# Pool fills an unread tile behind each indirect transfer while the chunks run; the scratch for dynamic transfers is halved

## The chip, the cores and the metric

The kernel runs on one core of one Trainium2 chip. The metric is the device time of the whole program in microseconds (us). PE is the matrix engine (TensorE), DVE the vector engine, ACT the scalar engine, POOL the GpSimd engine; SP issues most of the plain DMA transfers, and POOL issues the indirect ones, whose rows are picked by indices that lie in SBUF.

## What is computed

A long convolution by FFT, gated by x, and then a routed expert layer over the resulting 45824 tokens of width 128 (four sequences of 11456):

```python
def _attn_ref(x, v, pos_emb, w1, w2):
    h_filt = (np.maximum(pos_emb @ w1, 0.0) @ w2) * window        # filter of length S
    u = x * v
    y = irfft(rfft(u, 2 * S) * rfft(h_filt, 2 * S))[:, :S]        # along the sequence
    return x * y

def _moe_ref(x, w_skip, w_gate, w1, w2):
    out = x.copy()
    do_compute = x @ w_skip > 0
    xc = x[do_compute]
    logits = xc @ w_gate                                          # 8 experts
    e_idx = np.argmax(logits, axis=1)
    gate_w = softmax(logits)[e_idx]
    for e in range(E):
        h = np.maximum(xc[mask_e] @ w1[e], 0.0)                   # 128 -> 1024
        y[mask_e] = gate_w[mask_e, None] * (h @ w2[e])            # 1024 -> 128
    out[do_compute] = xc + y
```

Everything is float32.

## The kernel before

The program has four stretches. `first_phase` multiplies x by v, makes the filter and does the first step of the forward transforms. `freq_phase` does the second step, the product in the frequency domain and the first step of the inverse. `out_phase` does the last inverse step in 32 **chunks** of three blocks each, gates the result, stores it to `out` in HBM, scores every token and works out its place in a list of its expert. `late_slots` runs the experts.

A **slot** is 256 tokens of one expert, in two halves of 128. A slot needs three kinds of indirect transfers, and POOL issues all of them:

- `name` (L652): its 256 row numbers are fetched from `lists` into `ids`. One transfer.
- `gather` (L686): its rows of `out` are fetched into a buffer `xt`, 129 numbers a row. Two transfers, one for each half.
- `store` (L757): its results in a buffer `o` are written back to the rows of `out`. Two transfers.

The 29 **early slots** (`early_slots`) run inside `out_phase`, beside the chunks: a generator yields after each piece of work, and the loop over chunk steps resumes it once or more in a step. `late_slots` runs the rest after the chunks, partly two slots at a time. The order on each engine is written out by this code (the schedule is manual), so every engine works through a fixed list. For an early slot that is: turn the gathered rows (`turn_high`, PE transposes at L740 into a PSUM tile `mh`), multiply by the expert's first weights (`up`, L751 to L753), ReLU on ACT (L774), multiply by the second weights (L823), gate (`gated`, DVE at L763), two stores on POOL, then the `name` and `gather` transfers of later slots. Between them stand the chunk's own instructions: the inverse step (L1066) and its gating (`xm`, DVE at L1067), PE transposes (L1079, L1093), scores (L1087, copied out by ACT at L1089), and the routing (L1132 to L1194).

```python
for n in range(s, min(s + GATHERS, XT - 1 + s)):    # how far gathers run ahead
    if n not in got and n in self.names:
        got[n] = self.gather(n, self.ids[:, n], pool, self.names[n])
```

A gather is so issued as soon as its slot is named and lies within 12 slots ahead. POOL has no other work than indirect transfers from the start of the chunks on.

The scratch for dynamic transfers is a part of SBUF that the program sets aside at the start of each partition; unless it is said otherwise it is 16384 bytes. The kernel's tiles lie behind it.

The functions that the change touches, and what calls them:

Of the kernel before, what the change touches and what calls it, by code (L numbers as in the profile page):

```python
# [12 lines left out]
F16 = mybir.dt.float16  # L13
# [45 lines left out]
NLATE = 64  # L59
NLAST = NEARLY + NLATE - NKNOWN  # L60
NTAB = 188


def units():
# [11 lines left out]
def tables():  # L76
# [70 lines left out]
        "cols": (col[:, None] < col[None, :]).astype(np.float16), "odd": odd.astype(np.float16),  # L147
        "iota": np.tile(np.arange(NTAB, dtype=f), (X.stop, 1)),
        "shift": at64(shift).astype(np.float16), "bump": at64(bump.reshape(E, 1)).astype(f),
# [3 lines left out]
class First:  # L153
# [42 lines left out]
    def store(self):  # L196

        for dst, xs in self.late:
            self.nc.sync.dma_start(dst, xs)
        self.late = []  # L200
# [115 lines left out]
def freq_phase(tc, nc, i, fi, zd, c3, spare, loads):  # L316
# [9 lines left out]
    with (  # L326
# [116 lines left out]
        for n in range(ALL + LAG):  # L443
# [18 lines left out]
            begin(n + 1, 0)  # L462
            step()
            store()
            if n < ALL:
                half(1)
# [5 lines left out]
            if n < ALL:  # L472
                nc.gpsimd.tensor_tensor(y[:, 1:], y[:, 1:], p1, ALU.add)  # L473
                nc.gpsimd.tensor_tensor(y[:, 2:], y[:, 2:], p2, ALU.add)  # L474
            back(2)
        store(nc.scalar)


class Experts:
# [7 lines left out]
    def __init__(self, tc, i, out, lists, mc, wf):  # L487
# [10 lines left out]
        nc.vector.memset(self.ones, 1.0)  # L498
        self.iota = mc.tile([nx, NTAB], F32, name="iota")
        nc.sync.dma_start(self.iota, i["iota"])  # L500
        self.first = mc.tile([nx, NTAB], F16, name="first")
        nc.vector.memset(self.first, 0.0)
# [15 lines left out]
        nc.sync.dma_start(self.parts, i["parts"].rearrange("p (a b) -> p a b", a=2))  # L518
        self.past = mc.tile([nx, NTAB], F32, name="past")
        nc.vector.memset(self.past, 0.0)  # L520
# [4 lines left out]
        nc.vector.memset(self.counts, 0.0)  # L525
        self.tab = mc.tile([1, NKNOWN + NTAB], I32, name="tab")
        self.total = mc.tile([1, 1], I32, name="total")
# [12 lines left out]
    def table(self, counts, last, base, limit, unit, pool, keep, ps):  # L540
# [3 lines left out]
        nc = self.nc  # L544
        mm = nc.tensor.matmul
        col = lambda name, dt=F32: pool.tile([X.stop, 1], dt, name=name)[X]
        NC1 = 2 * E + 1
        shift, incl = self.shift[X, 0], self.shift[X, 1]
# [3 lines left out]
        mm(ps[X, C:C + 1], shift, done, start=True, stop=True)  # L552
        mm(ps[0:C, NTAB:NTAB + NC1], counts, self.sums[:, 0:NC1], start=True, stop=True)
        yield
# [89 lines left out]
    def sum(self, ps, pool, name="at"):  # L644
        at = pool.tile([128, 1], I32, name=name)
        with self.nc.allow_low_precision(reason="whole numbers that float32 holds"):
            self.nc.vector.tensor_reduce(at, ps, axis=AX.X, op=ALU.add)  # L647
        return at

    def name(self, at, ids, have=H2):  # L650

        self.nc.gpsimd.indirect_dma_start(  # L652
            out=ids, out_offset=None, in_=self.lists[0:have * PP],
            in_offset=bass.IndirectOffsetOnAxis(ap=at, axis=0), bounds_check=have * PP - 1, oob_is_err=False)

    def issue(self, one):
        s, at, ch = one
        self.name(at, self.ids[:, s], ch + 1)
        self.names[s] = ch

    def group(self, ins, name, *others):

        for g in others:
            self.tc.declare_no_dep(ins.ins, group=g, reason="they have rows of their own")
        self.tc.add_to_no_dep_group(name, ins.ins)
# [12 lines left out]
    def gather(self, s, ids, pool, since=None):  # L678

        nc = self.nc  # L680
        tb = self.entry(s, pool)
        self.held = (self.held + 1) % len(self.xts)
        xt = self.xts[self.held]
        have = 128 * NS * (H2 if since is None else since + 1)
        for j in range(2):
            ins = nc.gpsimd.indirect_dma_start(  # L686
                out=xt[:, j], out_offset=None, in_=self.rows[0:have],
                in_offset=bass.IndirectOffsetOnAxis(ap=ids[:, j:j + 1], axis=0),
                bounds_check=have - 1, oob_is_err=False)
            self.group(ins, "gathers", "outs", *(f"rows{c}" for c in self.stored if since is not None and c > since))  # L690
        return tb, xt, ids, since

    def space(self, pool):


        nc = self.nc
        self.xts, self.held = [pool.tile([128, 2, W], F32, name=f"xt{k}", bufs=1) for k in range(XT)], 0
        self.o, self.at = [pool.tile([128, 2, W], F32, name=f"o{k}", bufs=1) for k in range(4)], 0
        for t in self.xts + self.o:
            nc.vector.memset(t, 0.0)  # L700
        self.reaches, self.turns = [pool.tile([LP + 1, T2], F16, name=f"reach{k}", bufs=1) for k in range(4)], 0
        for t in self.reaches:
            nc.vector.memset(t, 0.0)
            nc.vector.tensor_copy(t[LP:], self.slotpos[LP:])
# [50 lines left out]
    def store(self, o, ids, j, since=None):  # L755
        nc = self.nc
        ins = nc.gpsimd.indirect_dma_start(  # L757
            out=self.rows, out_offset=bass.IndirectOffsetOnAxis(ap=ids[:, j:j + 1], axis=0),
            in_=o, in_offset=None, bounds_check=H2 * 128 * NS - 1, oob_is_err=False)
        self.group(ins, "outs", "outs", "gathers", *(f"rows{c}" for c in self.stored if since is not None and c > since))  # L760

    def gated(self, o, y, xt, j):
        self.nc.vector.scalar_tensor_tensor(o, y, xt[:, j, D:D + 1], xt[:, j, 0:D], ALU.mult, ALU.add)  # L763

    def early_slots(self, pool, work, psum, bank):
# [25 lines left out]
        def prepare(s):  # L791

            while not all(n in self.names for n in unit(s)):
                yield
            gather(s)
            if s not in hl:
                for _ in range(4):
                    yield
                    gather(s)
                w[s] = self.split(got[s][0], pool, 0, nc.vector)  # L800
                hl[s] = self.turn([got[n] for n in unit(s)], pool, bank512())
                yield
                yield
# [31 lines left out]
    def late_slots(self, pool, queue):  # L835
# [3 lines left out]
        nc, tc = self.nc, self.tc  # L839
        with (  # L840
# [40 lines left out]
            def leave(sts, yt):  # L881
# [4 lines left out]
                for n, (tb, xt, ids, since) in enumerate(sts):  # L886
                    o = self.row()
                    for j in range(2):
                        self.gated(o[:, j, 0:D], tp[:, n * T + j * 128:n * T + (j + 1) * 128], xt, j)
                        self.store(o[:, j], ids, j)  # L890

            st, w, h = self.ahead
            w1, hl = {0: w.pop(NEARLY)}, {0: h.pop(NEARLY)}
            count = len(UNITS)
# [100 lines left out]
def out_phase(tc, i, out, zd, ex, consts):  # L995
# [6 lines left out]
    with (  # L1002
# [3 lines left out]
      with (  # L1006
# [267 lines left out]
        for ch in range(NCH):  # L1274
            for blk in range(NB):
                for lag, rank, f in ((0, 0, produced), (1, 4, turn), (2, 4.9, score), (3, 2, score2), (STORE, 9, store)):
                    steps.setdefault(first(ch) + blk + lag, []).append((rank, f, (ch, blk)))
            for lag, order, f in (
                    (6, 3, choose), (7, 1, exp), (7, 4.5, count), (7, 6, counted), (7, 6, gate), (8, 4.4, total),
                    (9, -2.5, even), (9, 0.5, spreadcounts), (9, 4.5, ranks),  # L1280
                    (10, -2, routed), (11, 3, spread), (12, 4.5, collect), (13, -3, write)):
                steps.setdefault(first(ch) + lag, []).append((order, f, (ch,)))
# [103 lines left out]

# [9 lines left out]
```

## Time and profile before

| | |
|---|---|
| three runs | 1799.66, 1805.27, 1805.89 us; median 1805.27 us |
| the profiled execution | 1805.72 us, of which the span of its instructions is 1803.8 us |
| busy share of the span | PE 88%, DVE 66%, POOL 56%, ACT 46% |
| indirect transfers | 186 gathers, 186 stores, 93 names |
| of these from 815 to 1340 us | 82 gathers, 58 stores, 60 names |

In the profile, a group's row gives line, engine, operation, out<-in, the count, then busy time and mean duration in ns, and behind the second bar the engine's idle time just before it with what ended it. In a row of the timeline stand the start, the duration, and in brackets the idle time before it and what ended it; "remote" stands there where the profile finds no recorded instruction that ended shortly before the release. A row of stretches gives for each engine the busy time and the number of instructions, then the granted clock of PE (1.00 is full speed), the busy share of the DMA engines and GB/s.

### The profile page before, as it was taken

The page shows a single profiled execution, that of the slowest core. Times are in us where ns is not written, and L with a number is a line of the kernel's source. Part 1 is how long each engine was busy: PE and PEld are TensorE (multiplying, and loading weights), DVE is VectorE, ACT ScalarE, POOL GpSimd, SP SyncE. Part 2 cuts the span into 40 slices and gives each one's busy share as a digit, 9 for nine tenths or more (in the row PEclk, how much of TensorE's full clock was granted, in tenths as well). Part 3 has the DMA queues.
Part 4 walks back from the last instruction along what each step waited for, and adds up shares of the span by engine and source line. Part 5 has one row for each costly group of instructions (what it writes and reads, how often), then busy time and mean ns, then how long its engine had stood idle before and what let it go on. Part 6 is the DMA issues. An engine that isn't in the chain of part 4 may idle for free. (4 is left out here: it accounts for less than half of the span.)

```text
span 1803.8 us, 26628 instructions
## 1 busy us (share of the span) xinstructions
PE 1589.3 (88%) x8528; PEld 1009.3 (56%) x8528; DVE 1198.3 (66%) x2524; ACT 822.6 (46%) x1740; POOL 1012.6 (56%) x664
## 2 busy tenths in 40 slices
PE   6987999999999999687789778979768898899897
PEld 2543444444444444234566556756656776787896
DVE  1326778887887999477566545756656665577685
ACT  3553545455454444233344334535424554455664
POOL 1005888888887888203453432234565676677563
PEclk9987999999999999899899889989889998999899
DMA  7999999999997898798566645755211111111110
GB/s 257 321 347 337 375 381 363 347 321 331 346 323 256 227 340 222 213 334 249 162 214 183 211 141 188 229 172 179 72 22 26 34 40 36 34 40 36 28 35 19
DMA packets 188665, 360.34 MB, mean 200 GB/s; under 512 B 54794, under 2 KB 128988, under 8 KB 188516
## 3 DMA queue, kind: packets, MB, share of 16 engines
q1 hardware_dynamic: 169484, 318.63, 52.6%
q0 software_dynamic: 18144, 38.67, 7.5%
q10 hardware_dynamic: 896, 1.32, 0.3%
q8 instruction: 69, 1.13, 0.3%
q14 instruction: 72, 0.59, 0.1%
HBM read 215.50 MB, written 144.11 MB: 199 GB/s over the span
## 5 line engine op out<-in xcount | busy, mean ns | idle before, releaser
L757 POOL DMA_INDIRECT out<-o,ids x186 | 210.8, 1133 | 352.7 <-DVE o L763 292.6
L413 PE MATMUL ps<-y,c 128*128 128x512 f32 x720 | 331.7, 597 | 2.1 <-POOL y L473 1.4
L473 POOL TENSOR_TENSOR y<-y,p 128x2048 f32<-128x2048 f32 x60 | 272.2, 4537 | 70.8 <-DVE p L402 70.8
L686 POOL DMA_INDIRECT xt<-out,ids x186 | 191.8, 1031 | 77.3 <-issue 50.9
L861 DVE SCALAR_TENSOR_TENSOR hh<-hp,hh 128x1024 fp32r<-128x1024 f32 x128 | 155.9, 1218 | 116.8 <-ACT hh L860 94.9
L413 PEld LDWEIGHTS ps<-y,c 128*128 128x128 f32 x720 | 133.3, 190 | 175.3 <-issue 155.0
L402 DVE TENSOR_TENSOR p<-xp,g 128x1024 f32<-128x1024 f32 x240 | 217.4, 947 | 0.0
L402 DVE TENSOR_TENSOR y<-xp,g 128x1536 f32<-128x1536 f32 x120 | 210.7, 1756 | 4.1
L860 ACT ACTIVATE hh<-hp 128x1024 fp32r<-128x1024 f32 x128 | 131.9, 1031 | 135.9 <-PE hp L753 51.2
L414 ACT COPY z<-ps 128x512 f32<-128x512 f32 x180 | 105.5, 586 | 178.7 <-PE ps L413 167.4
L652 POOL DMA_INDIRECT ids<-lists,at x93 | 101.0, 1086 | 125.1 <-DVE at L647 97.7
L751 PE MATMUL hp<-hl,ws 128*128 128x512 f32 (+1 forms) x336 | 126.4, 376 | 28.3 <-DVE hh L861 13.3
L728 DVE TENSOR_TENSOR ws<-wf,ws 128x1024 fp32r<-128x1024 f32 x113 | 137.5, 1217 | 12.7 <-ACT ws L723 7.1
L474 POOL TENSOR_TENSOR y<-y,p 128x1024 f32<-128x1024 f32 x60 | 141.4, 2357 | 4.7
L823 PEld LDWEIGHTS bank<-wd,h 128*128 128x128 f32 x928 | 122.0, 212 | 36.5 <-issue 36.5
L823 PE MATMUL bank<-wd,h 128*128 128x128 f32 x928 | 133.3, 302 | 1.1 <-issue 1.1
L1066 PE MATMUL y<-zt,c 128*64 128x512 f32 x384 | 115.4, 665 | 15.7 <-issue 9.5
L1067 DVE TENSOR_TENSOR xm<-y,ox 128x512 f32<-128x512 f32 x96 | 66.5, 692 | 93.6 <-PE y L1066 47.5
L211 PE MATMUL ps<-wf,c 60*120 60x384 f32 x512 | 112.4, 534 | 11.6 <-DVE wf L194 11.2
L382 PE MATMUL xp<-x,wf 128*128 128x480 f32 x256 | 115.7, 576 | 7.1 <-issue 3.8
L723 ACT CAST ws<-wf 128x1024 fp32r x113 | 118.0, 1044 | 7.3 <-issue 1.8
L752 PE MATMUL hp<-hl,ws 128*128 128x512 f32 (+1 forms) x336 | 118.1, 351 | 1.0 <-issue 1.0
(188 smaller groups left out, 3102.9 us busy)
## 6 DMA issues: line engine op xcount, KB each, us to landing
wf<-xv SPq DMA_DIRECT2D x64, 768.0 KB
zt<-zd SPq DMA_DIRECT2D x64, 768.0 KB
x1d<-wf SPq DMA_DIRECT2D x64, 720.0 KB
x<-x1d SPq DMA_DIRECT2D x60, 768.0 KB
zd<-z SPq DMA_DIRECT2D x118, 384.0 KB
out<-xm SPq DMA_DIRECT2D x96, 258.0 KB
ox<-xo SPq DMA_DIRECT2D x96, 256.0 KB
x1f<-fx POOLq DMA_DIRECT2D x16, 720.0 KB
```

The costliest lines, as they stand in the source:

```text
L402: nc.vector.tensor_tensor(o[:, :, :, j * KH:(j + 1) * KH].rearrange("p s a k b d -> p (s a) k b d"), x[:, None].broadcast_to([128, m, KH, ...
L413: nc.tensor.matmul(zps, c3[:, a, :], y[:, blk, a], start=(a == 0), stop=(a == 1))
L473: nc.gpsimd.tensor_tensor(y[:, 1:], y[:, 1:], p1, ALU.add)
L474: nc.gpsimd.tensor_tensor(y[:, 2:], y[:, 2:], p2, ALU.add)
L686: ins = nc.gpsimd.indirect_dma_start(out=xt[:, j], out_offset=None, in_=self.rows[0:have], in_offset=bass.IndirectOffsetOnAxis(ap=ids[:, j ...
L728: eng.tensor_tensor(w[:, 1], src[:, ds(self.where(eng, tb), F)], w[:, 0].bitcast(F32), ALU.subtract)
L751: nc.tensor.matmul(hp, w[:, 0, c], hl[:, 0], start=True, stop=False)
L752: nc.tensor.matmul(hp, w[:, 0, c], hl[:, 1], start=False, stop=False)
L757: ins = nc.gpsimd.indirect_dma_start(out=self.rows, out_offset=bass.IndirectOffsetOnAxis(ap=ids[:, j:j + 1], axis=0), in_=o, in_offset=Non ...
L823: nc.tensor.matmul(bank[:, j * D:(j + 1) * D], h[f // 2][:, f % 2, j * 128:(j + 1) * 128], wd[s][:, f * D:(f + 1) * D], start=(f == 0), st ...
L860: nc.scalar.activation(h[:, 0], hp, AF.Relu)
L861: nc.vector.scalar_tensor_tensor(h[:, 1], hp, 0.0, h[:, 0].bitcast(F32), ALU.max, ALU.subtract)
```

## The change

A method `pause` has POOL fill a tile `idle` of 128 partitions x 512 half-precision numbers with zeros. Nothing reads that tile. `pause` is called behind every `name`, `gather` and `store` transfer, as long as the flag `apart` is set: it is set at the start of `out_phase` and cleared near the start of `late_slots`, ahead of the first late fetch. The scratch for dynamic transfers is set to 8192 bytes, half of what it was.

```diff
+IDLE = 512
 ...
         self.nc.gpsimd.indirect_dma_start(
             out=ids, out_offset=None, in_=self.lists[0:have * PP], ...)
+        self.pause()
+
+    def pause(self):
+
+        if self.apart:
+            self.nc.gpsimd.memset(self.idle, 0.0)
 ...
             self.group(ins, "gathers", "outs", ...)
+            self.pause()
         return tb, xt, ids, since
 ...
+        self.idle, self.apart = pool.tile([128, IDLE], F16, name="idle", bufs=1), True
         self.reaches, self.turns = [pool.tile(...) for k in range(4)], 0
 ...
         self.group(ins, "outs", "outs", "gathers", ...)
+        self.pause()
 ...
+            self.apart = False
             st, w, h = self.ahead
 ...
-    nc = bacc.Bacc("TRN2", target_bir_lowering=False, num_devices=1)
+    nc = bacc.Bacc("TRN2", target_bir_lowering=False, num_devices=1, dynamic_dma_scratch_size=8192)
```

The order of instructions on PE, DVE, ACT and SP stays as it was, and so do their waits but for a few on ACT. On POOL 207 fills are added, 67 behind names, 82 behind gathers and 58 behind stores. The first fill waits for PE once (its memory was used before); every other one waits for the fill before it.

POOL in the middle of the chunks, before: the stores of an early slot, a name, the gathers of three slots ahead, two names, and the next slot's stores. `o`, `xt` and `at` are the buffers of results, gathered rows and list positions; L757 is a store, L686 a gather, L652 a name.

```order
L757 DMA out<-o_4457,ids 49152x129 x2
L652 DMA ids<-lists,at_8131 128x2
L686 DMA xt_4446<-out,ids 128x129 x2
L686 DMA xt_4447<-out,ids 128x129 x2
L686 DMA xt_4448<-out,ids 128x129 x2
L652 DMA ids<-lists,at_8209 128x2
L652 DMA ids<-lists,at_8211 128x2
L757 DMA out<-o_4458,ids 49152x129 x2
```

The same place after, as far as the second gathered slot. The lines of the code have moved: L766 is a store, L693 a gather, L653 a name, L661 the fill.

```order
L766 DMA out<-o_4457,ids 49152x129
L661 MEMSET idle 128x512
L766 DMA out<-o_4457,ids 49152x129
L661 MEMSET idle 128x512
L653 DMA ids<-lists,at_8204 128x2
L661 MEMSET idle 128x512
L693 DMA xt_4446<-out,ids 128x129
L661 MEMSET idle 128x512
L693 DMA xt_4446<-out,ids 128x129
L661 MEMSET idle 128x512
L693 DMA xt_4447<-out,ids 128x129
L661 MEMSET idle 128x512
```

Nothing changes places; a fill stands behind each transfer.

POOL where the late slots begin, before: two names, then the first late fetches and stores.

```order
L652 DMA ids<-lists,at_12690 128x2
L652 DMA ids<-lists,at_12692 128x2
L686 DMA xt_4442<-out,ids 128x129 x2
L757 DMA out<-o_4457,ids 49152x129 x2
L757 DMA out<-o_4458,ids 49152x129 x2
```

The same place after:

```order
L661 MEMSET idle 128x512
L653 DMA ids<-lists,at_12876 128x2
L661 MEMSET idle 128x512
L653 DMA ids<-lists,at_12878 128x2
L661 MEMSET idle 128x512
L693 DMA xt_4442<-out,ids 128x129 x2
L766 DMA out<-o_4457,ids 49152x129 x2
L766 DMA out<-o_4458,ids 49152x129 x2
```

The last fill stands behind the last name that `out_phase` issues; from there on POOL's list is as before.

## The prediction

> **What bounds the kernel now.** I read the page's busy times first, then the rows of stretches for the stretch that the change touches, then the same rows cut at the early slots, and last the timeline of the worst of them.
>
> ```profile
> PE 1589.3 (88%) x8528; PEld 1009.3 (56%) x8528; DVE 1198.3 (66%) x2524; ACT 822.6 (46%) x1740; POOL 1012.6 (56%) x664
> 815.00:1340.00 525.00, 427.28 (x3622) 318.41 (x3622) 320.97 (x1239) 218.81 (x519) 211.99 (x200) 0.91 0.55 172
> 1340.00:1803.00 463.00, 410.57 (x2276) 351.32 (x2275) 305.87 (x456) 239.59 (x293) 291.64 (x266) 0.95 0.13 32
> ```
>
> In a row of a stretch the length comes first, then busy time of PE, PEld, DVE, ACT and POOL, PE's granted clock, the DMA share and GB/s. PE is the bound: 88% of the span. The chunks with the early slots run from about 815 to 1340 us, where PE is idle 525 − 427.3 = 97.7 us and its clock is granted at 0.91. POOL is busy 212 us there, all of it with indirect transfers, and idle 313.
>
> Where PE's time goes is seen when the stretch is cut at the first transposes of successive early slots (L740). The first three rows below are slots whose seven or eight transfers stand apart; the next is the same work with two transfers; the last seven are the slots with bursts.
>
> ```profile
> 1222.28:1238.61 16.33, 14.65 (x132) 10.74 (x132) 10.74 (x44) 7.91 (x19) 7.30 (x8) 1.00 0.60 180
> 1238.61:1254.01 15.40, 14.28 (x132) 10.58 (x131) 10.64 (x43) 7.71 (x19) 7.60 (x7) 1.00 0.66 219
> 1254.01:1269.61 15.60, 13.80 (x132) 10.54 (x131) 10.46 (x41) 8.07 (x20) 7.64 (x8) 1.00 0.22 69
> 1154.58:1169.28 14.70, 14.70 (x138) 10.78 (x139) 12.78 (x50) 7.49 (x19) 2.55 (x2) 1.00 0.72 236
> 860.42:883.88 23.46, 16.93 (x135) 12.41 (x135) 12.34 (x48) 8.11 (x19) 12.41 (x12) 0.93 0.60 190
> 883.88:903.87 19.99, 18.08 (x133) 12.95 (x134) 10.66 (x43) 7.91 (x19) 4.01 (x4) 0.74 0.41 118
> 937.02:959.54 22.52, 17.67 (x126) 12.60 (x126) 10.06 (x34) 7.94 (x19) 11.91 (x12) 0.84 0.57 180
> 1004.75:1029.07 24.32, 14.13 (x131) 10.52 (x131) 12.48 (x49) 7.64 (x19) 15.63 (x15) 0.89 0.67 198
> 1029.07:1053.55 24.48, 16.31 (x128) 12.40 (x128) 10.36 (x35) 8.06 (x20) 9.05 (x9) 0.78 0.50 140
> 1053.55:1074.08 20.53, 15.33 (x121) 11.82 (x121) 7.85 (x28) 7.75 (x20) 7.12 (x7) 0.89 0.42 140
> 1182.69:1207.60 24.91, 14.13 (x133) 10.47 (x132) 12.93 (x57) 7.74 (x20) 14.40 (x13) 0.87 0.58 178
> ```
>
> With two transfers a slot takes 14.70 us and PE never rests. With 15 or 13 transfers in it, it takes 24.3 or 24.9 us, although PE's own work is the same 14.1 us. The two in which PE is busy longer and POOL little (883.88, 1053.55) stand behind a burst and run at a clock of 0.74 and 0.89.
>
> The timeline inside the slot of 1004.75 shows how the time is lost, in order of start (start, duration, instruction, then idle time before it and what ended it):
>
> ```profile
> 1013.33 1.02 POOL L757 DMA_INDIRECT out<-o,ids  x1 [3.08 <-DVE o L763]
> 1015.83 0.43 PE L1087 MATMUL bank<-xT,wg 128*32 128x128 f32 x8
> 1016.19 1.08 PE L1066 MATMUL y<-zt,c 128*64 128x512 f32 x4
> 1019.93 1.00 POOL L686 DMA_INDIRECT xt<-out,ids  x1 [0.30 <-issue]
> 1023.41 0.27 ACT L1089 COPY lt<-bank 128x128 f32<-128x128 f32 x1 [5.10 <-remote]
> 1024.85 0.69 DVE L1067 TENSOR_TENSOR xm<-y,ox 128x512 f32<-128x512 f32 x1 [5.49 <-remote]
> 1026.44 1.12 POOL L652 DMA_INDIRECT ids<-lists,at  x1 [0.30 <-issue]
> 1028.42 0.60 ACT L774 ACTIVATE h<-mh 128x512 f32<-128x512 f32 x1 [4.69 <-remote]
> 1029.07 0.69 PE L740 MATMUL mh<-ident,xt 128*128 128x128 f32 x2 [10.19 <-ACT h L774]
> ...
> 1019.00:1023.80 4.80, 0.00 (x0) 0.00 (x0) 0.23 (x2) 0.32 (x2) 3.62 (x4) 1.00 0.53 133
> 1023.80:1034.00 10.20, 4.93 (x30) 4.52 (x31) 4.70 (x12) 3.55 (x8) 3.11 (x3) 0.50 0.77 244
> ```
>
> The copy `lt` and the gating `xm` read what PE had made by 1016.3 and 1017.3, and start some seven us later, each with about 5 us of idle time ended by "remote": no instruction of an engine. The ReLU `h`, for which PE then waits, is held in the same way. From 1019 to 1023.8 PE does nothing and POOL issues transfers at its fastest: 1.00 us busy, 0.30 us gap, so 0.77 a us. Then PE runs at half clock for 10 us. What hands PE's results on is thus late while POOL issues transfers back to back; what that is, the trace doesn't say.
>
> It speaks for transfers, not for POOL as such, that POOL's own arithmetic in the frequency stage leaves PE alone (POOL 86%, PE full):
>
> ```profile
> 300.00:400.00 100.00, 99.91 (x279) 43.29 (x278) 80.39 (x100) 49.56 (x130) 86.39 (x30) 1.00 0.97 338
> ```
>
> **The change part by part.** Price of a fill: the trace has two of POOL, and no fill of half-precision.
>
> ```profile
> masks.py:197 POOL MEMSET ident<- 128x128 f32 x1 | 0.2, 203 | 0.0
> L1389 POOL MEMSET const-float32-0.0<- 128x1 f32 x1 | 0.1, 98 | 0.2 <-issue 0.2
> L686 POOL DMA_INDIRECT xt<-out,ids x82 | 83.8, 1021 | 45.5 <-issue 21.0 <-DMA ids<-lists,at 17.1 <-ACT hl L742 3.1
> L757 POOL DMA_INDIRECT out<-o,ids x58 | 63.5, 1095 | 231.2 <-DVE o L763 210.1 <-DVE me L1111 12.3 <-issue 4.3
> L652 POOL DMA_INDIRECT ids<-lists,at x60 | 65.2, 1087 | 115.0 <-DVE at L647 97.7 <-issue 15.8 <-DVE to L1165 0.3
> ```
>
> From 1 to 128 elements a partition costs 203 − 98 = 105 ns, 0.83 ns an element, so 512 elements take 98 + 425 = 523 ns: 0.52 us. If two-byte elements go at half the price it is 0.31. The fill may lie in the 0.30 us gap that stands behind a transfer anyway (as little as 0.01 more), or bring a gap of its own (0.82). I take 0.52, by the two rows of the same operation. For 207 fills that is 108 us of POOL (2 to 170).
>
> Cover: POOL's 313 us of idle time, most of which is waiting for `o` (210.1) and for `at` (97.7). It is gone where POOL is the next to be waited for: at the end of the chunks, below.
>
> ```profile
> 1269.61:1340.00 70.39, 48.81 (x408) 43.09 (x409) 41.34 (x190) 23.57 (x45) 39.93 (x39) 0.86 0.16 44
> PE mh L740 <- DMA xt<-out,ids: 3.7, 2, 1.9
> ```
>
> 39 transfers at 1.30 + 0.52 = 1.82 us would take 71.0 of its 70.4 us: POOL would be full there. PE waits for gathered rows only 3.7 us in the whole stretch, since gathers run slots ahead. For the few just-in-time chains (a name, its landing, its gather, at the first slots and at the handoff) I put eight fills on the path, 4 us. Bounds: 0 if the lead of the gathers hides all, 20 us (39 × 0.52) if the whole handoff stands in POOL's order.
>
> Gain: the stake first. The seven burst slots sum to 160.21 us. At the mean of the three slots with seven or eight spread transfers, (16.33 + 15.40 + 15.60) / 3 = 15.78, they would take 110.4: a stake of 49.8 us. The stretch from 1269.61 adds at most 15 of its 21.6 idle us. The fill lowers POOL's pace in a burst from 1 / 1.30 = 0.77 to 1 / 1.82 = 0.55 transfers a us; the harmless slots have 8 / 16.33 = 0.49 on the mean, the burst slots 15 / 24.32 = 0.62 and 0.52 with pieces at 0.77. So the pace comes close to the harmless one and does not reach it. A straight line between 0.77 and 0.49 would give (0.77 − 0.55) / (0.77 − 0.49) = 0.79 of the stake, 39 us; but the mean of the harmless slots hides short pieces at 0.77, so that the run's length counts too, and the fill makes each run longer. I take about half, 26 us. Bounds: 65 (stake and tail) and −25 (second rival).
>
> Scratch for dynamic transfers: nothing seen waits for it.
>
> ```profile
> q0 software_dynamic: 18144, 38.67, 7.5%
> ```
>
> 18144 packets for 465 indirect transfers are 39 each, or 2.4 for each of 16 engines. No POOL row above waits for room. Half the room costs 0; the other way, the bound is the 15.8 us that names wait at issue, doubled. The moved addresses of the tiles and ACT's changed waits have no price in any row: 0.
>
> Sum: 1805.72 − 26 + 4 = 1783.7 for the profiled execution, which lies 0.45 over the median of the runs: 1783.
>
> What a rule says. Row first: the clock is granted at 1.00 until PE has been without work from 1019 to 1023.8, and then at 0.50 for 10.2 us. The Trainium skill, "TensorE: Matmul & The Clock Gate", section "Part 1: The HAM clock gate", has the clock fall to half after at least one idle window of about 3.4 us, and rise after a busy one; the trace agrees. By that rule a stall need only be cut under a window for the half-clock time behind it to vanish too, which would make the first rival the likelier.
>
> Against the change: the row below groups 83 small operations of DVE with a scalar, 277 ns each.
>
> ```profile
> L638 DVE TENSOR_SCALAR reach<-slotpos,spot 33x128 f16<-33x128 f16 x83 | 17.2, 277 | 0.0
> ```
>
> The Trainium skill, "SBUF — State Buffer", section "Who interferes with whom", lets a two-port operation of DVE (a copy or one with a scalar) and an instruction of POOL block each other wholly. An estimate from that page: fills cover 108 of the 525 us, so 17 of the 83 would meet one and wait half of it, 4.5 us of DVE in all, more if other operations of DVE are of that kind; DVE has 525 − 321 = 204 us idle there. No run yet shows it, and it is not in the sum.
>
> **The rivals.**
>
> 1. The stalls go altogether. For it: they are long only at 0.77, and half of their price is the slow clock that follows an idle piece of 4.8 us; a stall of under 3 us would not have it. Against it: 0.55 is still above 0.49. Time: 1805.7 − 50 + 3 = 1759.
>
> 2. Slower: the stall lasts as long as POOL's run of transfers does, at whatever pace, so that a longer run stalls longer. The place is the seven burst slots. The run gets 0.52 / 1.30 = 40% longer; half of the 49.8 us as stall proper gives +20 us, with the handoff's 4 some +25: 1830. It decides as soon as a stall ends with the run's end and not by pace. For it: `h` is released at 1028.4, 0.9 us behind the end of the run's last transfer (1026.44 + 1.12). Against it: `lt` is released at 1023.4, with the run still going, and the slots with shorter runs lose next to nothing.
>
> 3. The loss goes with the number of transfers, or the descriptors that they make, and not with their spacing: 15 still cost 10 us, 8 cost 1. Then only the fills' 4 us show: 1809, within the bound. The fill vanishing in the 0.30 us gap (the change does not do what it says) comes out the same. For it: time lost rises with the count in the rows (2, 8, 12, 15 transfers: 14.7, 15.8, 23.5, 24.3); against it, 13 cost more than 15.
>
> 4. POOL is late: gathers miss their slots at the handoff (20 us) and stores hold up the names: 1805.7 + 20 = 1826. For it the 39 transfers above; against it 3.7 us of waiting for rows.
>
> **How the numbers follow.** A chance of 0.32 for the forecast, 0.20 for the first rival, 0.16 for the second, 0.24 for the third (0.02 of it the vanishing fill), 0.08 for the fourth. Half a per cent, 9 us, is about what a measurement of this kernel can tell from no change. The first two are faster: 0.52; the third is the same: 0.24; second and fourth are slower: 0.24. The likeliest case's own range is 1766 to 1797 (gain 40 to 9, by the straight line and by the bound). With both signs in play the whole range goes from 1748 (stake and part of the tail) to 1832 (the second rival with two us over).
>
> **What the profile after would show.** The forecast is right if 207 fills of about 0.5 us stand on POOL; the slots with 12 to 15 transfers take 18 to 21 us instead of 23 to 25; "remote" idle time shrinks but stays; PE's clock in the stretch rises from 0.91 to about 0.95 and its idle time falls from 98 to about 75. The first rival: slots near 16 us, no stretch of half clock. The second: the same rows at 27 us and more. The third: unchanged slots with longer runs of POOL. The fourth: PE's wait for gathered rows above 15 us. It is wrong if a fill takes several times 0.5 us, or if the late stretch, which has no fills, moves by more than a few us.

## The result, and the profile after

| | before | after |
|---|---|---|
| median of four runs | 1804.6 us (1799.66 to 1805.89) | 1718.9 us (1707.4 to 1721.9) |
| ratio, 95% interval | | 0.954 [0.949, 0.960] |
| the profiled execution | 1805.72 us | 1707.4 us, the fastest of the four |

The changed kernel is 86 us faster, where 22 were forecast. The page's busy times after:

```profile
PE 1558.3 (91%) x8528; PEld 989.1 (58%) x8528; DVE 1219.0 (71%) x2524; ACT 822.8 (48%) x1740; POOL 1142.7 (67%) x871
```

POOL has its 207 instructions and 130 us more, DVE 21 us more with the same 2524 instructions, and PE 31 us less with the same 8528. For what follows the program is cut at PE's first transposes of a slot: **the early stretch** from the first slot to the 22nd (21 slots beside the chunks), **the handoff** over the last 8 early slots and the first 16 late ones, and **the late stretch** over the next 45 late slots, where the change has no fills. These three before, in rows of stretches (length, busy time of PE, PEld, DVE, ACT and POOL, PE's clock, DMA share, GB/s):

```profile
830.90:1207.60 376.70, 310.85 (x2611) 228.29 (x2611) 224.42 (x827) 159.79 (x387) 141.42 (x134) 0.91 0.62 192
1207.60:1435.34 227.74, 189.29 (x1270) 151.51 (x1271) 143.26 (x445) 99.20 (x169) 123.10 (x115) 0.92 0.23 67
1435.34:1762.49 327.15, 298.87 (x1676) 257.05 (x1674) 221.51 (x323) 176.59 (x217) 219.39 (x201) 0.95 0.14 35
```

And after:

```profile
833.42:1132.26 298.84, 290.94 (x2613) 213.35 (x2611) 237.34 (x829) 160.06 (x386) 207.95 (x253) 0.99 0.77 240
1132.26:1355.82 223.56, 188.23 (x1271) 151.93 (x1271) 152.48 (x452) 99.58 (x169) 181.23 (x203) 0.92 0.26 74
1355.82:1665.64 309.82, 290.22 (x1675) 252.49 (x1674) 221.86 (x324) 177.31 (x217) 223.24 (x198) 0.97 0.14 37
```

The early stretch gives 77.9 of the 98 us between the two profiled executions. There PE's idle time fell from 65.9 to 7.9 us and its busy time by 19.9, with the clock up from 0.91 to 0.99: no pause, and so no slow clock behind one. The handoff gives 4. The 17 us of the late stretch look like this execution's luck: the other three executions took 9 to 14 us longer than this one, and a second profile of the changed kernel (below, 1720.9 us) has 328.1 us there.

POOL in the chunks after, its timeline and the group of the fills:

```profile
985.58 1.00 POOL L653 DMA_INDIRECT ids<-lists,at  x1 [0.16 <-issue]
986.58 0.54 POOL L661 MEMSET idle<- 128x512 f16 x1
987.28 1.00 POOL L653 DMA_INDIRECT ids<-lists,at  x1 [0.16 <-issue]
988.28 0.54 POOL L661 MEMSET idle<- 128x512 f16 x1
988.99 1.03 POOL L766 DMA_INDIRECT out<-o,ids  x1 [0.17 <-DVE to L1176]
```

```profile
L661 POOL MEMSET idle<- 128x512 f16 x207 | 112.1, 541 | 0.2
```

A fill takes 0.54 us and begins as its transfer ends; the gap ahead of the next transfer shrank from 0.30 to 0.16 us. So transfers stand 1.00 + 0.54 + 0.16 = 1.70 us apart, against 1.30. Between 860 and 1200 us no "remote" wait of 2 us or more is left (the kernel before has 11 in its early stretch), although POOL has runs of up to 39 transfers there. In the late slots, where transfers stand 1.30 us apart as before, the pauses stay. One of them, with the last transfer ahead of it:

```profile
1337.03 1.00 POOL L693 DMA_INDIRECT xt<-out,ids  x1 [0.30 <-issue]
1340.53 1.02 ACT L870 ACTIVATE hh<-hp 128x1024 fp32r<-128x1024 f32 x1 [11.39 <-remote]
1342.86 0.79 PE L760 MATMUL hp<-hl,ws 128*128 128x512 f32 x1 [8.42 <-DVE hh L871]
```

ACT gets PE's result 2.5 us after POOL's run has ended, and PE has idled for 8.4. In all profiles with pauses, every "remote" wait of 2 us or more ends with an update of PE's own semaphore, the counter by which PE tells the others that it is done. The profile's ends of matmuls are modelled, so it can't tell whether the matmul itself was late or only its signal; "handed on late" stands for either below.

### The profile page after: what moved, and what is told of

It reads as the page before. It is cut to its first block, busy times and chain, and to the rows that moved or that the text cites. A ratio compares the mean times of both kernels' runs of the same rounds, so it can differ in the third digit from the quotient of the medians.

```text
span 1705.6 us, 26835 instructions
## 1 busy us (share of the span) xinstructions
PE 1558.3 (91%) x8528; PEld 989.1 (58%) x8528; DVE 1219.0 (71%) x2524; ACT 822.8 (48%) x1740; POOL 1142.7 (67%) x871
## 5 line engine op out<-in xcount | busy, mean ns | idle before, releaser
L766 POOL DMA_INDIRECT out<-o,ids x186 | 208.0, 1118 | 151.6 <-DVE o L773 111.1
L693 POOL DMA_INDIRECT xt<-out,ids x186 | 210.2, 1130 | 62.7 <-issue 37.2
L653 POOL DMA_INDIRECT ids<-lists,at x93 | 104.1, 1120 | 109.7 <-DMA zt<-zd 84.4
L1077 PE MATMUL y<-zt,c 128*64 128x512 f32 x384 | 110.9, 641 | 18.4 <-issue 9.2
L833 PEld LDWEIGHTS bank<-wd,h 128*128 128x128 f32 x928 | 109.4, 194 | 30.9 <-issue 30.8
L214 ACT COPY wf<-ps 120x384 f32<-120x384 f32 x256 | 105.7, 494 | 29.6 <-PE ps L212 28.5
L833 PE MATMUL bank<-wd,h 128*128 128x128 f32 x928 | 119.7, 283 | 0.0
```

The source lines that it names most:

```text
L693: ins = nc.gpsimd.indirect_dma_start(out=xt[:, j], out_offset=None, in_=self.rows[0:have], in_offset=bass.IndirectOffsetOnAxis(ap=ids[:, j ...
L766: ins = nc.gpsimd.indirect_dma_start(out=self.rows, out_offset=bass.IndirectOffsetOnAxis(ap=ids[:, j:j + 1], axis=0), in_=o, in_offset=Non ...
L833: nc.tensor.matmul(bank[:, j * D:(j + 1) * D], h[f // 2][:, f % 2, j * 128:(j + 1) * 128], wd[s][:, f * D:(f + 1) * D], start=(f == 0), st ...
```

## The experiments

The experiments ran on six chips, called A to F here. The kernel before was timed on each, and that is the first finding:

| chip | A | B | C | D | E | F |
|---|---|---|---|---|---|---|
| the kernel before, us | 1651.8 | 1650.2 | 1653.2 | 1649.6 | 1801.7 | 1787.8 |

A to D are called calm. E and F are like the chip of the prediction. All runs are of one execution, but for two on B that say otherwise.

**Four parts of it, on chip A.** The halved scratch alone (`dynamic_dma_scratch_size=8192` in the kernel before); the fill cut to 16 elements (`IDLE = 16`); twelve fills behind every twelfth transfer:

```diff
         if self.apart:
-            self.nc.gpsimd.memset(self.idle, 0.0)
+            self.passed += 1
+            if self.passed % 12 == 0:
+                for k in range(12):
+                    self.nc.gpsimd.memset(self.idle, 0.0)
```

and the fills kept on in the late slots (`self.apart = False` taken out).

> The kernel before with only the scratch halved, no fills. Theory 'spacing' (what counts is that transfers on POOL stand further apart) and theory 'instruction between' (what counts is that any other POOL instruction stands between two transfers): as before, 1800 to 1810 us, with the 5 us and longer 'remote' pauses of ACT and DVE in the chunk stretch and PE's clock at about 0.91 there. Theory 'scratch' (the smaller scratch or the moved addresses did it): about 1720 us, PE idle under 25 us between 860 and 1190.

> The changed kernel with a fill of 16 elements instead of 512. In the changed kernel a transfer, its fill and the gap behind take 1.01 + 0.54 + 0.16 = 1.71 us; with a fill of about 0.11 us it would be 1.28 us, the pace of before (1.30). Theory 'spacing': the stalls come back, 1795 to 1810 us. Theory 'instruction between': 1705 to 1725 us, no 'remote' pause over 3 us in the chunk stretch, at a pace as fast as before.

> The changed kernel's fills in groups: twelve fills in a row behind every twelfth transfer, none behind the others, so that POOL has as many transfers and fills as after the change (its mean pace is the same) but transfers stand back to back at 1.30 us up to twelve at a time. Theory 'spacing' in its form 'mean pace over tens of us': 1710 to 1735 us. 'Spacing from one transfer to the next' and 'instruction between': the runs of 9 to 12 stall PE again, 1760 to 1800 us, and the pauses lie inside the runs of 7 and more transfers without a fill.

> The changed kernel with the fills kept on in the late slots, some 215 more. The profile after has PE pauses of 7.6, 8.4, 3.9, 3.9 and 4.9 us in the late slots, behind runs of 9 to 39 transfers at 1.30 us. 'Spacing' and 'instruction between': these pauses go (some 30 us and the half-clock windows behind them, 15 us), against which POOL gets 215 x 0.42 = 90 us more work in a stretch where it is busy two thirds: 1680 to 1710 us if PE stays the bound, 1720 to 1740 if POOL becomes it. Rival 'the pauses of the late slots have another cause' (waits on ACT or on rows): they stay, 1720 or more.

Measured, in this order: 1652.1, 1639.9, 1678.5 and 1764.1 us, against 1651.8 for the kernel before. No theory had a kernel before at 1652, so the first three told nothing about the pauses: none of the four profiles has a "remote" wait of 2 us in the early, handoff or late stretch. In the profile of the scratch alone, POOL runs 142 transfers on end, 1.33 us apart on the mean, and PE, in the row of that stretch, is busy for every microsecond of it at full clock:

```profile
1275.00:1464.00 189.00, 189.00 (x894) 156.06 (x893) 140.12 (x207) 109.59 (x128) 145.55 (x142) 1.00 0.17 45
```

Back-to-back transfers alone are thus not enough for pauses: the chip, or its state at the time, has to do with it. The late fills told one thing that holds anyhow. They make POOL the bound of the late stretch, with 340 of 375 us busy and PE waiting; its row:

```profile
1335.39:1710.15 374.76, 312.29 (x1676) 267.33 (x1674) 224.75 (x324) 178.50 (x217) 340.20 (x406) 0.92 0.12 32
```

**The changed kernel on calm chip B**, beside the fill of 16 and the scratch again; the first two timed in ten runs each, the kernel before in 19.

> The changed kernel itself, timed once more beside the kernel before. In the four runs before this one the kernel before took 1652 us on its chip, against 1805 on the chip of the prediction, with no 'remote' pause although POOL ran up to 142 transfers back to back. Theory 'the chip' (back-to-back transfers hold up the handing on of results only on some chips or at some times, and the change only takes that away): where before takes about 1652, the changed kernel takes 1645 to 1670, no gain, since POOL only does more; where before takes about 1805, it takes about 1719. Rival 'the fills gain by themselves' (the order in which transfers start, less crowding of the transfers): the changed kernel is faster by 3% or more on any chip.

> The fill of 16 elements again, timed in rounds. It keeps the pace of transfers (1.28 us each) and puts an instruction between them. Where before takes about 1652: 1640, so 0.7% less, if the one run of before was no accident; 1652 if it was. Where before takes about 1805: 'spacing' says 1795 to 1810, 'instruction between' 1640 to 1725.

> The halved scratch alone, again. On a chip where before takes about 1805 'scratch' says 1720 and every other theory 1800 to 1810; on one where it takes 1652, 1652.

The changed kernel took 1648.3 us against 1650.2: ratio 0.9995 [0.998, 1.001], no gain and no loss. The fill of 16: 1644.5 us, 0.9975 [0.996, 0.999], a small gain at most. The scratch: 1643.8 in one run. "The chip" holds, "the fills gain by themselves" falls: all of the gain is the pauses' going. The calm profile of the halved scratch alone, which is the kernel before in all else, gives the yardstick for the three stretches:

```profile
836.03:1128.82 292.79, 287.65 (x2610) 211.60 (x2611) 222.87 (x821) 158.79 (x385) 136.91 (x128) 1.00 0.77 244
1128.82:1320.87 192.05, 178.24 (x1272) 144.87 (x1271) 144.50 (x452) 99.23 (x169) 132.81 (x124) 0.98 0.30 87
1320.87:1601.74 280.87, 280.10 (x1675) 247.70 (x1674) 221.16 (x324) 175.54 (x217) 213.28 (x195) 1.00 0.15 40
```

Against it the pauses cost the kernel before 376.7 − 292.8 = 83.9 us in the early stretch, 35.7 in the handoff and 46.3 in the late stretch. The change takes back 77.9 of the first. The same kernel's profile on A has 296.8, 195.6 and 280.9 us in the three, so the first two losses are good to some 4 us.

**Fills to the end, of 16 and of 128 elements** (B), **and of 256 in the chunks alone** (C): `IDLE` changed, and for the first two the late `self.apart = False` taken out.

> Fills of 16 elements (0.13 us, a pace of 1.31 us a transfer as without fills) behind every transfer, in the late slots too. On a chip where the kernel before takes about 1650: 1640 to 1655, since the pace stays and POOL has 215 x 0.01 us more to do. Where it takes about 1805: theory 'instruction between' says 1640 to 1670 (all pauses gone, in the late slots too), theory 'spacing' 1790 to 1810 (nothing gained, since the pace is as before).

> Fills of 128 elements in the late slots too: about 0.13 + 112 x 0.83 ns = 0.22 us each, a pace of about 1.40 us. POOL is nearly full from 1275 to 1625 us in the kernel before on a calm chip, and 512-element fills in the late slots cost 112 us there (215 x 0.42 = 90 by the sum). By that sum 128 elements cost 215 x 0.10 = 22 us: 1660 to 1680 where before takes about 1650; if POOL is not the bound at this pace, 1645 to 1655. Where before takes about 1805: 'instruction between' 1665 to 1690, 'spacing' (1.40 lies near 1.30) 1760 to 1800.

> Fills of 256 elements in the chunks only (about 0.33 us each, a pace of about 1.50 us a transfer, between 1.31 and 1.71). Where the kernel before takes about 1650: 1643 to 1655, as with 16 and with 512 elements, no 'remote' pause. Where it takes about 1805: 'instruction between' about 1719, as with 512; 'spacing' 1730 to 1770, part of the way.

1646.8, 1666.1 and 1648.8 us, as expected of calm chips. 128 elements to the end cost 16 us by POOL in the late stretch alone (296.7 us against 280.9).

**More transfers instead of fills** (D): behind every second transfer of the chunks another gather, from an input into unread tiles.

```diff
-        if self.apart:
-            self.nc.gpsimd.memset(self.idle, 0.0)
+        self.passed += 1
+        if self.apart and self.passed % 2:
+            more = self.idles[self.passed // 2 % 8]
+            self.nc.gpsimd.indirect_dma_start(
+                out=more, out_offset=None, in_=self.source, in_offset=bass.IndirectOffsetOnAxis(ap=self.zeros, axis=0), ...)
```

> No fills; instead, behind every second transfer of the chunks, one transfer more: 128 rows of 128 numbers of an input, into tiles that nothing reads (some 104 transfers, 8 tiles in turn). The pace within a run is that of before, 1.30 us, and the runs and the number of transfers are half as large again. Where the kernel before takes about 1650: theory 'the chip' says no 'remote' pause over 2 us even so, and a time of 1650 to 1675 (POOL is later at the end of the chunks). Rival 'the number of transfers' (a calm chip only has some room more): pauses return in the chunk stretch, 1680 to 1800. Where it takes about 1805: 1810 to 1850 by either.

1687.6 us against 1649.6, above the 1675 expected, but with no "remote" pause; the longest run has 90 transfers in the chunks, and PE stays at full clock:

```profile
855.00:980.00 125.00, 121.73 (x1107) 89.65 (x1106) 96.05 (x360) 68.06 (x163) 98.18 (x89) 1.00 0.79 250
```

Most of the 38 us lies in the late stretch, which has none of the added transfers and takes 311.8 us against 280.9: POOL is late there, as in the fourth rival, and its 207 transfers fill the stretch without a rest. The worst single wait is 12 us at the first late slots, behind DVE, which waits for a store to land:

```profile
1306.84 0.79 PE L768 MATMUL hp<-hl,ws 128*128 128x512 f32 x1 [12.27 <-DVE hh L879]
```

So the number of transfers doesn't bring pauses on a calm chip. A second run of 16 elements to the end on D took 1641.0 us.

**A chip with pauses, E**: 16 elements to the end, and the scratch alone.

> Fills of 16 elements behind every transfer to the end of the program, on another chip. Before at about 1650: 1640 to 1655 again. Before at about 1805: 'spacing' and 'scratch' leave the late pauses as they are; 'spacing' says 1790 to 1810, 'instruction between' 1640 to 1670, 'scratch' 1720 to 1735.

> The halved scratch alone, on the same chip as the run before this one. Before at about 1650: 1642 to 1655. Before at about 1805: 'scratch' 1720, the others 1800 to 1810.

1788.0 and 1810.0 us against 1801.7. "Scratch" falls. Its early stretch has the clock and the idle time of the kernel before:

```profile
836.59:1206.94 370.35, 308.08 (x2611) 226.29 (x2611) 224.59 (x828) 159.78 (x386) 141.04 (x134) 0.92 0.63 196
```

So does "instruction between". With a fill of 16 behind each transfer, the early stretch is hardly shorter:

```profile
829.32:1188.47 359.15, 305.48 (x2610) 223.23 (x2611) 225.81 (x833) 159.38 (x387) 158.63 (x268) 0.94 0.64 203
```

And its timeline has the old pause in a run whose transfers have fills between them and stand 1.31 us apart:

```profile
1015.07 1.00 POOL L693 DMA_INDIRECT xt<-out,ids  x1 [0.18 <-issue]
1016.07 0.13 POOL L661 MEMSET idle<- 128x16 f16 x1
1016.37 1.00 POOL L653 DMA_INDIRECT ids<-lists,at  x1 [0.18 <-issue]
1019.95 0.69 DVE L1077 TENSOR_TENSOR xm<-y,ox 128x512 f32<-128x512 f32 x1 [5.31 <-remote]
```

**What spacing is needed, on chip F**: 256 elements to the end, groups of twelve, 256 in the chunks, and the changed kernel.

> Fills of 256 elements (0.33 us, some 1.50 us a transfer) in the chunks and the late slots. Where the kernel before takes about 1650: by late128's 16 us for 0.10 us a transfer and late512's 112 for 0.42, about 1690, with POOL over 90% busy in the late slots. Where it takes about 1800: 1690 to 1730 if 1.50 us is spacing enough, with no pause over 4 us anywhere; 1740 to 1780 if it is not.

> Twelve fills of 512 elements behind every twelfth transfer of the chunks. Where the kernel before takes about 1650: 1675 to 1680, as the first time. Where it takes about 1800: 'spacing from one transfer to the next' says that the runs of 7 to 12 pause PE as before, 1780 to 1830; 'mean pace' 1720 to 1750.

> Fills of 256 elements in the chunks alone. Where the kernel before takes about 1650: 1643 to 1655. Where it takes about 1800: between the 1788 of the 16 elements and the 1719 of the 512; a straight line over the pace (1.31, 1.50, 1.71 us) gives 1755, a threshold above or below 1.50 one of the two ends.

> The changed kernel on the same chip as the three before it. Where the kernel before takes about 1650: 1644 to 1654. Where it takes about 1800: 1705 to 1722, as on the chip of the prediction.

1700.7, 1797.6, 1716.3 and 1720.9 us against 1787.8. The early stretch of the groups of twelve, which have nearly as many fills of 512 as the change (192 against 207):

```profile
835.79:1186.81 351.02, 305.39 (x2611) 223.28 (x2611) 226.90 (x815) 158.38 (x386) 200.79 (x251) 0.94 0.65 204
```

And a pause in one of their runs, from the timeline:

```profile
1024.02 1.02 POOL L770 DMA_INDIRECT out<-o,ids  x1 [0.30 <-issue]
1025.34 1.00 POOL L770 DMA_INDIRECT out<-o,ids  x1 [0.30 <-issue]
1027.11 0.69 DVE L1082 TENSOR_TENSOR xm<-y,ox 128x512 f32<-128x512 f32 x1 [3.22 <-remote]
```

At most twelve transfers at 1.30 us with some 6.5 us of fills behind them still pause PE: 58 of the 84 us lost in the early stretch are lost here too. So the mean pace over a dozen isn't what decides; the spacing from one transfer to the next is. The early stretch with 256 elements and with 512, a row of each kernel:

```profile
837.33:1143.60 306.27, 290.49 (x2611) 212.64 (x2611) 227.48 (x821) 158.65 (x385) 180.60 (x256) 0.99 0.74 233
```

```profile
834.11:1130.63 296.52, 289.68 (x2612) 212.16 (x2611) 237.27 (x829) 159.93 (x386) 207.26 (x253) 0.99 0.77 242
```

With 256 (0.33 us, transfers 1.50 us apart) the "remote" waits of 2 us and more are gone from the stretch too, and 10 us of mostly small waits are left. By pace, with the three stretches of each kernel on a chip with pauses:

| between transfers | kernel (chip) | early | handoff | late |
|---|---|---|---|---|
| 1.30 us | scratch alone (E) | 370.3 | 225.4 | 335.8 |
| 1.30, groups of twelve | (F) | 351.0 | 242.0 | 327.1 |
| 1.31 | 16, to the end (E) | 359.2 | 223.3 | 333.8 |
| 1.50 | 256, chunks (F) | 306.3 | 204.9 | 326.1 |
| 1.50 | 256, to the end (F) | 308.2 | 197.0 | 318.6 |
| 1.70 | 512, chunks: the change (F) | 296.5 | 220.3 | 328.1 |
| calm chip, 1.30 | scratch alone (B) | 292.8 | 192.1 | 280.9 |

Between 1.31 and 1.50 us the long pauses go. (1.31 was run on E and 1.50 on F; on F itself the rows to compare are the groups of twelve, 1.50 and 1.70.) 256 elements to the end is the fastest on a chip with pauses, 20 us under the change: its late stretch has no "remote" wait of 2 us, its early one a single one of 3.2. But POOL is nearly full there, as its row shows (284 of 319 us), and little of the 46 us comes back:

```profile
1338.64:1657.26 318.62, 291.63 (x1675) 253.37 (x1674) 223.51 (x324) 176.42 (x217) 283.85 (x398) 0.97 0.14 36
```

DVE waits there for POOL's stores to land, and PE for DVE (us in all, times, longest):

```profile
DVE o L773 <- DMA out<-o,ids: 48.1, 43, 2.2
PE hp L760 <- DVE hh L871: 21.5, 11, 3.4
```

On a calm chip it wasn't run; between the 16 us that 128 elements and the 112 us that 512 cost there, it would lose some 50, an estimate by a straight line over the fill's duration (0.22, 0.33 and 0.54 us). No kernel tried is the best on both kinds of chip.

## Why the prediction was wrong

**Direction and mechanism were right**, on a chip with pauses. PE's results are handed on late while POOL issues transfers at its fastest, and wider spacing takes that away. The third rival (number) and the second (a longer run pauses longer) fell; so did the fourth, since the changed kernel costs nothing on a calm chip.

**The step that failed most is "I take about half, 26 us".** It put a straight line between the pace of a run (0.77 a us) and the mean pace of the harmless slots (0.49), got 39 us, and lowered that to 26 for the runs' length. The effect isn't a straight line over the pace: 1.31 us apart is nearly as bad as 1.30, at 1.50 the long pauses are gone, and length doesn't count once the spacing is there (39 transfers in a run without one). The seven burst slots fell from 160.2 to 100.9 us. The mean of a slot was the wrong scale, as the groups of twelve show. The first rival, "the stalls go altogether", is what happened.

**The second was the stake, 49.8 us.** It measured seven burst slots against 15.78 us, the mean of three "harmless" slots of the same profile. These three lie behind the 21 of the early stretch and are long by themselves. The calm profile of the scratch alone (B) has 45.57 us for the three together, against 47.33 before, and 100.00 for the seven burst slots, the sum of their rows:

```profile
1141.44:1187.01 45.57, 42.26 (x393) 31.67 (x393) 31.93 (x124) 23.33 (x57) 23.37 (x22) 1.00 0.55 171
sum 100.00, PE 98.46 PEld 72.88 DVE 75.33 ACT 54.54 POOL 67.78; mean PE 14.07 PEld 10.41 DVE 10.76 ACT 7.79 POOL 9.68
```

So the seven lost 60.2 us, not 49.8, and the other 14 slots, which the stake put at nothing, lost 23.7 more: 83.9 in all 21. A slot takes 292.8 / 21 = 13.94 us on that calm chip and 298.84 / 21 = 14.23 after the change. The prediction's own rows had the better yardstick: PE's busy time of 14.13 us in the slots of 1004.75 and 1182.69, and the slot of 14.70 with no idle time. At 14.13 us all 21 slots would take 296.7 us, a stake of 80. With a loss of that size the first rival's time would have been 1726 (1805.7 − 83.9 + 4), 7 us from the result, and the range would not have ended at 1748.

**The tail added next to nothing.** "At most 15" of the stretch from 1269.61 was in the bound; the handoff gave 4 us, since the pauses stay in its late slots.

**Smaller terms.** A fill: 0.52 forecast, 0.541 measured. The gap behind it: 0.30 in the sum, in fact 0.16. Just-in-time chains, 4 us: on the calm chip the whole change costs −1 us, give or take 3. Scratch, 0: 1652.1 against 1651.8, 1643.8 against 1650.2 and 1810 against 1802, one execution each. A late stretch that "moves by more than a few us" was named as a sign of being wrong: it is 17 us shorter in the profiled execution and 1 us longer in the second profile, so nothing hangs on it.

**The two rules.** The clock was granted at 0.91 in the early stretch before and at 0.99 after, with its last stretch of half clock from 837 us on: 20 of the 78 us are the slow clock that no longer follows. "TensorE: Matmul & The Clock Gate", section "Part 1: The HAM clock gate", in the Trainium skill lets the clock fall after an idle window of some 3.4 us. The traces have it fall behind less. Before, it fell where PE was busy for 1.26 of 3.41 us and idle for at most 2.25 us on end:

```profile
1102.32:1105.73 3.41, 1.26 (x7) 0.25 (x5) 1.05 (x6) 1.85 (x3) 2.24 (x3) 1.00 0.50 135
1105.73:1109.14 3.41, 3.30 (x15) 3.30 (x16) 0.69 (x1) 1.52 (x4) 0.00 (x0) 0.50 0.10 19
```

After, at the start of the early stretch, it fell where PE was busy for 2.03 of 3.41 us and idle for at most 1.25 us on end:

```profile
834.00:837.41 3.41, 2.03 (x23) 1.29 (x23) 2.80 (x15) 2.20 (x7) 0.00 (x0) 1.00 0.97 304
837.41:844.23 6.82, 6.71 (x32) 4.21 (x30) 6.38 (x25) 3.18 (x6) 4.62 (x6) 0.50 0.47 132
```

So to cut each pause under 3 us, the first rival's reason, would not have been enough here. Behind 844 us PE is idle for 6 us in all of the early stretch, and no half clock is left in it.

Beside the fills, several of DVE's operations with one input got longer, and those with two inputs hardly. Three groups before:

```profile
L1165 DVE TENSOR_SCALAR to<-rs 128x12 int32<-128x12 f32 x28 | 4.9, 176 | 1.0
L1105 DVE TENSOR_TENSOR df<-lg,mx 128x96 f32<-128x96 f32 x27 | 7.0, 258 | 0.9
L647 DVE TENSOR_REDUCE at<-bank 128x1 int32<-128x2 f32 x81 | 8.9, 152 | 6.6 <-remote 4.9 <-PE mh L753 1.2 <-PE y L1066 0.3
```

And after, with `reach` as a fourth:

```profile
L1176 DVE TENSOR_SCALAR to<-rs 128x12 int32<-128x12 f32 x28 | 9.3, 332 | 1.0
L1116 DVE TENSOR_TENSOR df<-lg,mx 128x96 f32<-128x96 f32 x27 | 7.0, 259 | 0.9
L648 DVE TENSOR_REDUCE at<-bank 128x1 int32<-128x2 f32 x93 | 12.8, 219 | 0.1
L639 DVE TENSOR_SCALAR reach<-slotpos,spot 33x128 f16<-33x128 f16 x93 | 24.5, 389 | 0.0
```

The first two groups and `reach` fit what the Trainium skill, "SBUF — State Buffer", section "Who interferes with whom", says of two-port operations, and of two inputs beside an instruction of POOL that only writes. The reduce `at` goes against that section, by which a reduce never contends on this chip; why it got longer stays open. The estimate from the section, 4.5 us for the `reach` group, was low: 93 × (389 − 277) = 10 us. Over all of DVE it is the 21 us of the profile's page. They cost no time that can be seen: on the calm chip the whole change made none.

## What to carry to other kernels

Where engines wait long for results that the profile shows as made long ago ("remote") while POOL issues indirect transfers on end, space the transfers out one by one: 1.5 us from start to start was enough here, 1.31 was not, and a pause behind each dozen helped little. Spend POOL's idle time on it, and stop where POOL has none: in the late slots even 128 elements cost 16 us on a chip that had no pauses. Size such a loss against the bound engine's own work at full clock, never against the better slots of the same profile, and time the kernel on more than one chip before tuning for a pause.

## What the runs showed of the hardware that was not expected

The same program takes 1650 us on four chips and 1788 to 1805 in three measurements elsewhere (two chips, and that of the prediction, which may be one of them); up to the first gathered slot the profiles agree within a few us, and the difference lies in the pauses and the slow clock behind them. What makes a chip one or the other stays open, and also whether a chip stays what it is: B was calm in two sets of runs ten minutes apart, each other chip was used once. No experiment brought the pauses to a calm chip, neither 142 transfers on end nor half as many transfers again in the chunks. Open too is what holds PE's results up, or PE itself. That the spacing decides rests, on the chips with pauses, on one execution of each kernel, with whole times 60 us and more apart; where between 1.31 and 1.50 us the border lies wasn't tried.
